# Zero-padding the first key tile of the value products, padding the first queries, and joining a unit's transposes in an attention + SwiGLU + SiLU kernel

## The chip, the cores and the metric

One core of one Trainium2 chip runs the whole program. The metric is the device time of one execution in microseconds (us); the kernel before has a median of 1140.44 us over three runs (1138.94 to 1141.12).

## What is computed

Three layers follow one another, all in float32.

- Forgetting attention with B = 4 batches, H = 8 heads, S = 576 positions, D = 64: `scores = q k^T / 8 + min(-(cum_i - cum_j), 0)` with `cum = cumsum(max(s, 0))`, a causal mask, a softmax, and the product with v.
- SwiGLU over the 2304 tokens x 512: `silu(x @ w_gate) * (x @ w_val) @ w_out` with an inner width of 1536.
- SiLU over the result: `silu(x @ w_in) @ w_out` with an inner width of 2048.

## The kernel before, in words

**Precision by parts.** Most matmuls run on operands of type fp32r, split into a high and a low part (`..h` and `..l`), so that one product is made of two or three matmuls. In the feed-forward layers these are lines 406 to 408 (high x high, high x low, low x high), always on the full array of 128 rows (contraction) by 128 columns (outputs), in spans of 288 tokens in the first layer. Only batch 0 keeps its attention weights whole in fp32 (`WHOLE_P`).

**Attention.** A sequence of 576 is cut into five tiles: the first has 64 positions, the others 128 (`TILES`). A unit is one half of one head: half A has the query tiles 0, 1, 2 (320 queries), half B the tiles 3 and 4 (256 queries). There are 64 units. Each goes through three stages, one slot apart:

- `a_scores` (L212), once per query tile: GpSimd makes the bias with its mask (L218, L221), TensorE the two score matmuls (L230; the first query tile has 64 queries and so a weight tile of 128 x 64), VectorE the sum with the minimum (L235), ScalarE the exponential (L241), and VectorE or GpSimd the normalization, into a buffer `e` (six of them).
- `a_transpose` (L250), once per group of key tiles (`GROUPS`: the first key tile alone, then tiles 1 and 2, then in half B tiles 3 and 4): transposes on TensorE (L264) of every query tile of the unit into one PSUM buffer `ptr`, then ScalarE takes the high part `ph` (L273) and VectorE the low part `pl` (L274). For the first key tile these have 64 rows.
- `a_pv` (L281): the value products (L292), two matmuls (`ph`, `pl`) for each key tile, all into one PSUM accumulator `pv`. The weights are the values with their high and low part side by side (128 columns): `vsa` for the first key tile, with 64 rows, `vsb` for the others, with 128. ScalarE and VectorE then join the two halves of the result (L306, L307).

PSUM has four buffers (`ps_a`) for all of attention's products: in each pair of slots scores, `pv` and `ptr` take 13 of them in turn, so that a tile takes over the buffer of the fourth one before it.

**Order.** After 18 slots of attention alone (batch 0 and a little of batch 1), chunks of the first feed-forward layer of batch b and slots of attention of batch b + 1 run interleaved: a chunk (`gv`, four steps of 24 matmuls, or `o1`, eight steps of 12) shares its steps out over the pieces of two slots (`slot_pieces`, L509). A slot's pieces are its scores, the split (L182) and load of the heads that follow, the value products of the unit two slots back, and the transposes of the unit one slot back, each group a piece of its own. The framework then fixes each engine's order at compile time, with a cost model of its own, so that it can put feed-forward matmuls ahead of a piece that would have to wait. In the first batch's chunks the weights are also decoded (`w_decode`, L364) on VectorE and ScalarE. The last batch's chunks and the second layer run without attention.

Of the kernel before, what the change touches and what calls it, by code (L numbers as in the profile page):

```python
# [8 lines left out]
F32 = mybir.dt.float32  # L9
F32R = mybir.dt.float32r  # L10
U32 = mybir.dt.uint32
AF = mybir.ActivationFunctionType
ALU = mybir.AluOpType
# [4 lines left out]
P = 128  # L18
# [49 lines left out]
def kernel(  # L68
# [15 lines left out]
    def pool(name, bufs, space=None, scope=ctx, side="left"):  # L84
        kw = {"space": space} if space is not None else {}
        return scope.enter_context(tc.tile_pool(name=name, bufs=bufs, side=side, reuse_waits="tile", **kw))
# [12 lines left out]
    qks_p = pool("qks", 2, scope=attention, side="right")  # L99
    cum_p = pool("cum", 2, scope=attention, side="right")  # L100
    e_p = pool("e", 6, scope=attention, side="right")
    pt_p = pool("pt", 4, scope=attention, side="right")
    v_p = pool("v", 2, scope=attention, side="right")
    xr_p = pool("xr", 2, scope=attention, side="right")
    xq_p = pool("xq", 2, scope=attention, side="right")
# [4 lines left out]
    def copy(eng, out, in_, scale=1.0):  # L110
        if eng == "a":
            nc.scalar.activation(out=out, in_=in_, func=AF.Copy, scale=scale)  # L112
        elif eng == "v":
            nc.vector.tensor_scalar(out=out, in0=in_, scalar1=scale, scalar2=None, op0=ALU.mult)
        else:
            nc.gpsimd.tensor_scalar(out=out, in0=in_, scalar1=scale, scalar2=1.0, op0=ALU.mult, op1=ALU.mult)
# [1 line left out]

    ident = const.tile([P, P], F32, name="ident")
    make_identity(nc, ident)  # L120
    cum = const.tile([B * H, S], F32, name="cum")
    cumq = const.tile([P, len(TILES), B * H], F32, name="cumq")
    cum_d = dram.tile([B * H, S], F32, name="cum_d")
    w32 = dram.tile([NGV + NO1, P, CW], F32, name="w32")
# [19 lines left out]


    st, loads = {}, []

    def a_load(b, h, halves):
        k1, v1, q0 = SPAN[halves]
# [28 lines left out]
    def a_split(b, h, halves):  # L178
        k1, v1, q0 = SPAN[halves]
        t, c, xa, xb = st.pop((b, h, halves))  # L180
        if (b, h) in WHOLE_S:
            ks, qs = t[:D, 1], (t[:D, 0],)  # L182
            q = t[:D, 0, q0:k1]
            nc.vector.tensor_scalar(out=q, in0=q, scalar1=-0.125, scalar2=None, op0=ALU.mult)
        else:
            ks = qks_p.tile([P, S], F32R, tag="ks", name="ks")
            qh = qks_p.tile([P, S], F32R, tag="qh", name="qh")
            ql = qks_p.tile([P, S], F32R, tag="ql", name="ql")
            qs = (qh, ql)
            copy(KHI[b], ks[:, :k1], t[:, 1, :k1])  # L190
            copy(QHI[b], qh[:, q0:k1], t[:, 0, q0:k1], -0.125)
            eng = nc.gpsimd if b in POOL_KS else nc.vector
            eng.tensor_tensor(out=ks[D:P, :k1], in0=t[D:P, 1, :k1], in1=ks[D:P, :k1].bitcast(F32), op=ALU.subtract)
            nc.vector.scalar_tensor_tensor(
                out=ql[:, q0:k1], in0=t[:, 0, q0:k1], scalar=-0.125, in1=qh[:, q0:k1].bitcast(F32),
                op0=ALU.mult, op1=ALU.subtract,
            )
        if (b, h) not in WHOLE_P:
            va_s = v_p.tile([64, 2, D], F32R, tag="vsa", name="vsa")
            vb_s = v_p.tile([P, 4, 2, D], F32R, tag="vsb", name="vsb")  # L200
            copy(VHI[b], va_s[:, 0, :], xa)
            copy(VHI[b], vb_s[:, :v1, 0, :], xb[:, :v1])
            nc.vector.tensor_tensor(out=va_s[:, 1, :], in0=xa, in1=va_s[:, 0, :].bitcast(F32), op=ALU.subtract)
            eng = nc.gpsimd if b in POOL_V else nc.vector
            eng.tensor_tensor(
                out=vb_s[:, :v1, 1, :], in0=xb[:, :v1], in1=vb_s[:, :v1, 0, :].bitcast(F32), op=ALU.subtract
            )
            xa, xb = va_s.rearrange("p t d -> p (t d)"), vb_s.rearrange("p j t d -> p j (t d)")
        for half in halves:
            st[b, h, half, "in"] = (ks, qs, c, xa, xb)  # L210

    def a_scores(b, h, half, i):  # L212
        ks, qs, c, _, _ = st[b, h, half, "in"]
        q0, r = TILES[i]
        wd = q0 + r
        hh = b * H + h
        e = e_p.tile([P, S], F32, tag="e", name="e")
        nc.gpsimd.tensor_scalar(  # L218
            out=e[:r, :wd], in0=c[:r, :wd], scalar1=-1.0, scalar2=cumq[:r, i, hh : hh + 1], op0=ALU.mult, op1=ALU.add
        )  # L220
        nc.gpsimd.affine_select(  # L221
            out=e[:r, q0:wd], in_=e[:r, q0:wd], pattern=[[-1, r]], compare_op=ALU.is_ge,
            fill=QMASK, base=0, channel_multiplier=1,
        )
        chunks = [(0, wd)] if wd <= 512 else [(0, wd // 2), (wd // 2, wd // 2)]
        m = None
        for c0, n in chunks:
            ps = ps_a.tile([P, 512], F32, tag="a", name="psc")
            for part, q in enumerate(qs):
                nc.tensor.matmul(  # L230
                    out=ps[:r, :n], lhsT=q[:, q0 : q0 + r], rhs=ks[:, c0 : c0 + n],
                    start=(part == 0), stop=(part == len(qs) - 1),
                )
            m2 = sm_p.tile([P, 1], F32, tag="m", name="m")
            nc.vector.tensor_tensor_reduce(  # L235
                out=e[:r, c0 : c0 + n], in0=ps[:r, :n], in1=e[:r, c0 : c0 + n], scale=1.0,
                scalar=3.0e38 if m is None else m[:r], op0=ALU.add, op1=ALU.min, accum_out=m2[:r],
            )
            m = m2
        l = sm_p.tile([P, 1], F32, tag="l", name="l")  # L240
        nc.scalar.activation(  # L241
            out=e[:r, :wd], in_=e[:r, :wd], func=AF.Exp, bias=m[:r], scale=-1.0, accum_out=l[:r]
        )
        rl = sm_p.tile([P, 1], F32, tag="rl", name="rl")
        nc.vector.tensor_scalar(out=l[:r], in0=l[:r], scalar1=1.0e-9, scalar2=None, op0=ALU.add)
        nc.vector.reciprocal(out=rl[:r], in_=l[:r])
        copy("v" if (b, i) in DVE_NORM else "g", e[:r, :wd], e[:r, :wd], rl[:r])
        st[b, h, "e", i] = e

    def a_transpose(b, h, half, js):  # L250
        tiles, base, n = HALF[half]
        ps = ps_a.tile([P, 512], F32, tag="a", name="ptr")
        kw = TILES[js[0]][1]
        at, put = 0, []
        for j in js:
            k0 = TILES[j][0]
            lo = max(k0, base)
            for i in tiles:
                q0, r = TILES[i]
                if q0 < k0:  # L260
                    continue
                e = st[b, h, "e", i]
                o = at + q0 - lo
                nc.tensor.transpose(ps[:kw, o : o + r], e[:r, k0 : k0 + kw], ident[:r, :r])  # L264
            put.append((j, at, lo - base, base + n - lo))
            at += base + n - lo
        ph = pt_p.tile([P, 512], F32 if (b, h) in WHOLE_P else F32R, tag="ph", name="ph")
        parts = (ph,)
        if (b, h) in WHOLE_P:
            copy("v" if (half, js[0]) in DVE_PT else "a", ph[:kw, :at], ps[:kw, :at])  # L270
        else:
            pl = pt_p.tile([P, 512], F32R, tag="pl", name="pl")
            nc.scalar.activation(out=ph[:kw, :at], in_=ps[:kw, :at], func=AF.Copy)  # L273
            nc.vector.tensor_tensor(  # L274
                out=pl[:kw, :at], in0=ps[:kw, :at], in1=ph[:kw, :at].bitcast(F32), op=ALU.subtract
            )
            parts = (ph, pl)
        for j, o, off, width in put:
            st[b, h, "p", half, j] = ([p[:kw, o : o + width] for p in parts], off, width)

    def a_pv(b, h, half):  # L281
        tiles, base, n = HALF[half]
# [226 lines left out]
    def slot_pieces(u):  # L509
        pcs = []  # L510
        if u < len(units):
            b, h, half, sp = units[u]
            for i in HALF[half][0]:
                pcs.append(lambda b=b, h=h, half=half, i=i: a_scores(b, h, half, i))
            if half == sp[0]:
                n = spans.index((b, h, sp))
                if n + 1 < len(spans):
                    pcs.append(lambda x=spans[n + 1]: a_split(*x))
                if n + 2 < len(spans):
                    pcs.append(lambda x=spans[n + 2]: a_load(*x))  # L520
        if u >= 2 and u - 2 < len(units):
            x = units[u - 2][:3]
            pcs.append(lambda x=x: a_pv(*x))
        if 1 <= u and u - 1 < len(units):
            b, h, half, _ = units[u - 1]
            for js in GROUPS[half]:
                pcs.append(lambda b=b, h=h, half=half, js=js: a_transpose(b, h, half, js))
        return pcs

    def w_ahead(c):  # L530
# [5 lines left out]

    def body():
        setup()
        a_load(*spans[0])
        a_load(*spans[1])  # L540
        a_split(*spans[0])
# [98 lines left out]
```

## Time and profile before

| | |
|---|---|
| median of three runs | 1140.44 us (1138.94 to 1141.12) |
| the profiled execution | 1141.18 us, of which the span from first to last instruction is 1139.4 us |
| busy in the span | TensorE 96%, VectorE 67%, GpSimd 54%, ScalarE 49% |
| chain that ended last | TensorE 73%, VectorE 6%, DMA 2%, issue 2%, ScalarE 1% |

How to read the rows further down: PE is TensorE's matmuls, PEld its weight loads, DVE is VectorE, ACT ScalarE, POOL GpSimd. A matmul's form is given as rows*columns of its weights, then the moving operand's shape: `64*128 64x320` contracts over 64 rows, gives 128 outputs, and streams 320 columns. Matmuls overlap and their ends are modelled, so what one costs is read from the start of one to the start of the next, not from its duration.

### The profile page before, as it was taken

The page shows a single profiled execution, that of the slowest core. Times are in us where ns is not written, and L with a number is a line of the kernel's source. Part 1 is how long each engine was busy: PE and PEld are TensorE (multiplying, and loading weights), DVE is VectorE, ACT ScalarE, POOL GpSimd, SP SyncE. Part 2 cuts the span into 40 slices and gives each one's busy share as a digit, 9 for nine tenths or more (in the row PEclk, how much of TensorE's full clock was granted, in tenths as well). Part 3 has the DMA queues.
Part 4 walks back from the last instruction along what each step waited for, and adds up shares of the span by engine and source line. Part 5 has one row for each costly group of instructions (what it writes and reads, how often), then busy time and mean ns, then how long its engine had stood idle before and what let it go on. Part 6 is the DMA issues. An engine that isn't in the chain of part 4 may idle for free.

```text
span 1139.4 us, 19549 instructions
## 1 busy us (share of the span) xinstructions
PE 1096.2 (96%) x6765; PEld 1000.2 (88%) x6765; DVE 764.8 (67%) x1776; ACT 561.0 (49%) x1242; POOL 615.9 (54%) x731
## 2 busy tenths in 40 slices
PE   7978988989999999999999999999999999999998
PEld 4656888888999999999999999889888898988887
DVE  6888998998877786777766435863463636454333
ACT  5876666655667655576744433455232323322221
POOL 4679889868877776686833543332333232223221
PEclk9988999999999999999999999999999999999999
DMA  5586565666343344333216222630111101000013
GB/s 141 136 244 215 175 193 189 182 173 196 119 119 113 109 117 144 113 101 101 69 54 217 75 84 84 202 109 25 50 51 43 57 19 56 19 1 1 1 51 116
DMA packets 53730, 121.41 MB, mean 107 GB/s; under 512 B 8256, under 2 KB 21568, under 8 KB 53632
## 3 DMA queue, kind: packets, MB, share of 16 engines
q1 hardware_dynamic: 53632, 120.17, 34.6%
q8 instruction: 53, 0.87, 0.3%
q14 instruction: 45, 0.37, 0.1%
HBM read 101.20 MB, written 18.95 MB: 105 GB/s over the span
## 4 chain that ended last, share of the span: by engine, by line
PE 73%; DVE 6%; DMA 2%; issue 2%; ACT 1%; POOL 0%; SPq 0%; DVEq 0%; ACTq 0%
PE po L406 9%; PE po L407 9%; PE po L408 9%; PE pgv L406 7%; PE pgv L407 7%; PE pgv L408 7%; PE pu L407 5%; PE pu L406 5%; PE pu L408 5%; PE pv L292 4%; PE ptr L264 3%; PE psc L230 2%; DVE dk L376 1%; DMA r<-in_w_dram 1%; DMA x2r<-x_d 1%
## 5 line engine op out<-in xcount | busy, mean ns | idle before, releaser
L421 POOL TENSOR_TENSOR h<-u,h 128x288 fp32r<-128x288 f32 (+2 forms) x176 | 187.1, 1064 | 332.5 <-ACT h L112 329.1
L406 PE MATMUL pgv<-xt,wh 128*128 128x288 f32 x768 | 233.7, 305 | 5.0 <-DVE u L417 3.5
L406 PE MATMUL po<-h,wh 128*128 128x288 f32 (+2 forms) x704 | 233.1, 333 | 3.7 <-DVE u L419 1.5
L407 PE MATMUL po<-h,wh 128*128 128x288 f32 (+2 forms) x704 | 232.6, 331 | 0.1
L408 PE MATMUL po<-h,wl 128*128 128x288 f32 (+2 forms) x704 | 232.3, 330 | 0.0
L408 PE MATMUL pgv<-xt,wl 128*128 128x288 f32 x768 | 230.0, 300 | 1.4 <-POOL wl L395 1.4
L407 PE MATMUL pgv<-xt,wh 128*128 128x288 f32 x768 | 230.0, 300 | 0.5 <-DVE xt L313 0.5
L395 POOL TENSOR_TENSOR wl<-wraw,wh 128x1024 fp32r<-128x1024 f32 x53 | 130.0, 2453 | 60.4 <-ACT wh L112 59.9
L406 PEld LDWEIGHTS pgv<-xt,wh 128*128 128x128 f32 x768 | 147.2, 192 | 6.7 <-DVE u L417 4.5
L408 PEld LDWEIGHTS pgv<-xt,wl 128*128 128x128 f32 x768 | 146.7, 191 | 1.8 <-POOL wl L395 1.8
L407 PEld LDWEIGHTS pgv<-xt,wh 128*128 128x128 f32 x768 | 147.1, 192 | 1.1 <-DVE xt L313 0.8
L218 POOL TENSOR_SCALAR e<-cumb,cumq 64x64 f32<-64x64 f32 (+4 forms) x160 | 112.4, 708 | 62.8 <-PE ptr L264 55.2
L406 PEld LDWEIGHTS po<-h,wh 128*128 128x128 f32 x704 | 132.0, 188 | 12.0 <-DVE u L419 2.0
L112 ACT ACTIVATE h<-u 128x288 fp32r<-128x288 f32 (+2 forms) x176 | 88.8, 508 | 102.2 <-DVE u L417 58.5
L408 PEld LDWEIGHTS po<-h,wl 128*128 128x128 f32 x704 | 132.2, 188 | 7.1
L407 PEld LDWEIGHTS po<-h,wh 128*128 128x128 f32 x704 | 132.2, 188 | 6.8 <-POOL h L421 0.5
L241 ACT ACTIVATE e<-e,m 64x64 f32<-64x64 f32 (+4 forms) x160 | 89.2, 558 | 95.9 <-DVE m L235 95.4
L417 DVE SCALAR_TENSOR_TENSOR u<-th,pu 128x464 f32<-128x464 f32 (+1 forms) x80 | 50.5, 631 | 122.3 <-ACT th L415 116.7
L501 DVE SCALAR_TENSOR_TENSOR acc<-po,acc 128x464 f32<-128x464 f32 (+1 forms) x140 | 88.7, 635 | 62.1 <-PE po L408 61.6
L415 ACT ACTIVATE th<-pu 128x464 f32<-128x464 f32 (+1 forms) x80 | 44.2, 552 | 174.0 <-PE pu L408 174.0
L112 ACT ACTIVATE wh<-wraw 128x1024 fp32r<-128x1024 f32 x88 | 92.2, 1053 | 56.0 <-PE po L407 32.1
L407 PE MATMUL pu<-x,wh 128*128 128x464 f32 (+1 forms) x320 | 118.9, 372 | 0.0
(83 smaller groups left out, 2189.3 us busy)
## 6 DMA issues: line engine op xcount, KB each, us to landing
wraw<-w SPq DMA_DIRECT2D x54, 512.0 KB, 4.0
r<-in_w_dram SPq DMA_DIRECT2D x52, 512.0 KB, 5.1
qkr<-in_qk_dram SPq DMA_DIRECT2D x64, 288.0 KB, 4.5
w<-wraw SPq DMA_DIRECT2D x18, 512.0 KB, 4.4
cumb<-cum_d SPq DMA_DIRECT2D x30, 288.0 KB, 3.4
r<-in_w_dram SPq DMA_DIRECT2D x32, 256.0 KB, 3.2
x_d<-acc SPq DMA_DIRECT2D x32, 144.0 KB, 3.8
vrb<-in_vb_dram SPq DMA_DIRECT2D x32, 128.0 KB, 3.6
```

Source lines behind the costliest of these rows:

```text
L112: nc.scalar.activation(out=out, in_=in_, func=AF.Copy, scale=scale)
L218: nc.gpsimd.tensor_scalar(out=e[:r, :wd], in0=c[:r, :wd], scalar1=-1.0, scalar2=cumq[:r, i, hh : hh + 1], op0=ALU.mult, op1=ALU.add)
L241: nc.scalar.activation(out=e[:r, :wd], in_=e[:r, :wd], func=AF.Exp, bias=m[:r], scale=-1.0, accum_out=l[:r])
L292: nc.tensor.matmul(out=acc[:rows, off : off + width], lhsT=vv, rhs=pp, start=(j == 0 and part == 0), stop=(j == js[-1] and part == len(ps) ...
L395: engines[eng].tensor_tensor(out=wl, in0=t, in1=wh.bitcast(F32), op=ALU.subtract)
L406: nc.tensor.matmul(out=ps[:, :n], lhsT=a, rhs=xh, start=(k == 0), stop=False)
L407: nc.tensor.matmul(out=ps[:, :n], lhsT=a, rhs=xl, start=False, stop=False)
L408: nc.tensor.matmul(out=ps[:, :n], lhsT=c, rhs=xh, start=False, stop=(k == last))
L415: nc.scalar.activation(out=th[:, :n], in_=pg[:, :n], func=AF.Tanh, scale=0.5)
L417: nc.vector.scalar_tensor_tensor(out=u, in0=th[:, :n], scalar=1.0, in1=pg[:, :n], op0=ALU.add, op1=ALU.mult)
L421: engines[LO[ph]].tensor_tensor(out=lo, in0=u, in1=hi.bitcast(F32), op=ALU.subtract)
L501: nc.vector.scalar_tensor_tensor(out=a, in0=ps[:, :n], scalar=0.5, in1=a, op0=ALU.mult, op1=ALU.add)
```

## The change

Four things are done. (1) For the batches whose weights are split, the first key tile's values (`vsa`) and weights (`ph`, `pl`) live in tiles of 128 rows whose upper 64 rows were filled with zeros once at the start by `zeros()` on GpSimd; the value products of that key tile then contract over 128 rows. These are three value tiles taken in turn and one pair of weight tiles for each half; the pool of the other `ph` and `pl` tiles has three buffers in place of four. (2) The score matmuls always take 128 query columns as weights, so the first query tile's do too, though only 64 rows of the result are read. (3) `a_transpose` issues all groups of a unit first and evicts them after, as one piece of the slot in place of two or three. (4) `cum` and the zeros' source `z` take buffers of the pool `e`.

```diff
-    pt_p = pool("pt", 4, scope=attention, side="right")
+    pt_p = pool("pt", 3, scope=attention, side="right")
+    zero_p = pool("zero", 1, scope=attention, side="right")
...
-    cum = const.tile([B * H, S], F32, name="cum")
+    cum = e_p.tile([B * H, S], F32, tag="e", name="cum")
...
+    first_v, first_p = [], []
+
+    def zeros():
+        z = e_p.tile([P, S], F32, tag="e", name="z")
+        nc.gpsimd.memset(z[D:P], 0.0)
+        for n in range(3):
+            va_s = zero_p.tile([P, 2, D], F32R, tag=f"v0_{n}", name="vsa")
+            copy("g", va_s[D:P], z[D:P, : 2 * D].rearrange("p (t d) -> p t d", t=2))
+            first_v.append(va_s)
+            if n == 2:
+                break
+            both = []
+            for part in "hl":
+                t = zero_p.tile([P, 320], F32R, tag=f"p{part}0_{n}", name=f"p{part}0")
+                copy("g", t[D:P], z[D:P, :320])
+                both.append(t)
+            first_p.append(both)
...
-            va_s = v_p.tile([64, 2, D], F32R, tag="vsa", name="vsa")
+            va_s = first_v[(b * H + h) % 3]
...
-            copy(VHI[b], va_s[:, 0, :], xa)
+            copy(VHI[b], va_s[:D, 0, :], xa)
...
-                    out=ps[:r, :n], lhsT=q[:, q0 : q0 + r], rhs=ks[:, c0 : c0 + n],
+                    out=ps[:, :n], lhsT=q[:, q0 : q0 + P], rhs=ks[:, c0 : c0 + n],
...
-    def a_transpose(b, h, half, js):
+    def a_transpose(b, h, half):
         tiles, base, n = HALF[half]
-        ps = ps_a.tile([P, 512], F32, tag="a", name="ptr")
...
+        done = []
+        for js in GROUPS[half]:
+            ps = ps_a.tile([P, 512], F32, tag="a", name="ptr")
...
+                    nc.tensor.transpose(ps[:kw, o : o + r], e[:r, k0 : k0 + kw], ident[:r, :r])
...
+            done.append((js, ps, kw, at, put))
+        for js, ps, kw, at, put in done:
+            whole = (b, h) in WHOLE_P
+            if js == (0,) and not whole:
+                ph, pl = first_p["AB".index(half)]
+                rows = P
...
+                st[b, h, "p", half, j] = ([p[:rows, o : o + width] for p in parts], off, width)
...
-            for js in GROUPS[half]:
-                pcs.append(lambda b=b, h=h, half=half, js=js: a_transpose(b, h, half, js))
+            pcs.append(lambda b=b, h=h, half=half: a_transpose(b, h, half))
...
         setup()
+        zeros()
```

## Rows read from the trace of the kernel before

**Rows 1.** Windows by stage: stretch, its length, busy us per engine (instructions).

```profile
0.00:118.00 118.00, 97.24 (x477) 69.11 (x477) 96.80 (x307) 82.27 (x209) 84.05 (x140) 0.91 0.65 185
118.00:262.00 144.00, 128.76 (x897) 119.10 (x896) 134.71 (x315) 86.35 (x199) 120.22 (x134) 0.98 0.62 185
262.00:608.00 346.00, 346.00 (x2559) 330.39 (x2558) 265.64 (x735) 209.09 (x513) 247.74 (x339) 1.00 0.37 111
608.00:1139.40 531.40, 524.20 (x2839) 481.64 (x2837) 267.65 (x423) 183.32 (x321) 163.88 (x120) 1.00 0.20 65
```

**Rows 2.** Chain that ended last by line, 262 to 608 us.

```profile
by line: PE pgv L406 15.5%; PE pgv L407 15.2%; PE pgv L408 15.2%; PE pv L292 13.5%; PE ptr L264 9.2%; PE po L406 7.8%; PE po L408 7.7%; PE po L407 7.7%; PE psc L230 7.4%; DMA x2r<-x_d 1.2%; DVE acc L449 0.1%; SPq L451 0.1%; issue 0.0%
```

**Rows 3.** Timeline of TensorE, half B's value products: start us, us, instruction.

```profile
525.95 0.29 PE L406 MATMUL po<-h,wh 128*128 128x288 f32 x1
...
526.22 0.29 PE L408 MATMUL po<-h,wl 128*128 128x288 f32 x1
526.43 0.38 PE L292 MATMUL pv<-ph,vsa 64*128 64x256 f32 x1
526.66 0.28 PE L292 MATMUL pv<-pl,vsa 64*128 64x256 f32 x1
526.86 0.38 PE L292 MATMUL pv<-ph,vsb 128*128 128x256 f32 x1
527.09 0.28 PE L292 MATMUL pv<-pl,vsb 128*128 128x256 f32 x1
...
527.56 0.28 PE L292 MATMUL pv<-pl,vsb 128*128 128x256 f32 x1
```

**Rows 4.** The same view, half A's value products, first and last.

```profile
262.83 0.29 PE L407 MATMUL pgv<-xt,wh 128*128 128x288 f32 x1
...
263.88 0.22 PE L292 MATMUL pv<-ph,vsb 128*128 128x128 f32 x1
```

**Rows 5.** The same, score matmuls of 320 columns.

```profile
534.56 0.31 PE L230 MATMUL psc<-ks,qh 128*128 128x320 f32 x1
534.70 0.31 PE L230 MATMUL psc<-ks,ql 128*128 128x320 f32 x1
```

**Rows 6.** Tile pv from 262 us: counts, min/median/max ns.

```profile
L292 PE MATMUL pv<-ph,vsa x36: 382/396/413, 263.1 to 600.8; 64*128 64x320 f32 x18, 64*128 64x256 f32 x18
```

**Rows 7.** Timeline of TensorE, the first query tile's scores.

```profile
388.04 0.19 PE L230 MATMUL psc<-ks,qh 128*64 128x64 f32 x1
...
388.34 0.29 PE L407 MATMUL pgv<-xt,wh 128*128 128x288 f32 x1
```

**Rows 8.** The same, the second query tile's scores.

```profile
280.61 0.25 PE L230 MATMUL psc<-ks,qh 128*128 128x192 f32 x1
...
280.96 0.29 PE L407 MATMUL po<-h,wh 128*128 128x288 f32 x1
```

**Rows 9.** The same, three transposes between feed-forward matmuls.

```profile
310.59 0.49 PE L264 MATMUL ptr<-ident,e 128*128 128x128 f32 x3
...
311.05 0.30 PE L407 MATMUL pgv<-xt,wh 128*128 128x288 f32 x1
```

**Rows 10.** The same, one transpose between feed-forward matmuls.

```profile
318.51 0.27 PE L264 MATMUL ptr<-ident,e 128*64 128x128 f32 x1
...
318.75 0.29 PE L408 MATMUL pgv<-xt,wl 128*128 128x288 f32 x1
```

**Rows 11.** Lines by form, GpSimd, first 12 us: count, busy, mean, idle before.

```profile
L218 POOL TENSOR_SCALAR e<-cumb,cumq 64x64 f32<-64x64 f32 x1 | 0.8, 753 | 7.0 <-ACT cumb L168 7.0
```

**Rows 12.** Timeline of all engines, value product's last matmul and its join.

```profile
282.63 0.28 PE L292 MATMUL pv<-pl,vsb 128*128 128x128 f32 x1
...
283.46 0.49 DVE L307 TENSOR_TENSOR x<-pv,xtmp 64x320 f32<-64x320 f32 x1
```

**Rows 13.** The same, another unit.

```profile
309.04 0.28 PE L292 MATMUL pv<-pl,vsb 128*128 128x128 f32 x1
...
313.78 0.41 DVE L307 TENSOR_TENSOR x<-pv,xtmp 64x256 f32<-64x256 f32 x1
```

More of the change, by code (lines that the diff above doesn't have):

```diff
@@ L198, in a_split @@
         if (b, h) not in WHOLE_P:
-            va_s = v_p.tile([64, 2, D], F32R, tag="vsa", name="vsa")
+            va_s = first_v[(b * H + h) % 3]
             vb_s = v_p.tile([P, 4, 2, D], F32R, tag="vsb", name="vsb")
-            copy(VHI[b], va_s[:, 0, :], xa)
+            copy(VHI[b], va_s[:D, 0, :], xa)
             copy(VHI[b], vb_s[:, :v1, 0, :], xb[:, :v1])
-            nc.vector.tensor_tensor(out=va_s[:, 1, :], in0=xa, in1=va_s[:, 0, :].bitcast(F32), op=ALU.subtract)
+            nc.vector.tensor_tensor(out=va_s[:D, 1, :], in0=xa, in1=va_s[:D, 0, :].bitcast(F32), op=ALU.subtract)
             eng = nc.gpsimd if b in POOL_V else nc.vector
@@ L248, in a_scores @@
         st[b, h, "e", i] = e
-    def a_transpose(b, h, half, js):
+    def a_transpose(b, h, half):
         tiles, base, n = HALF[half]
-        ps = ps_a.tile([P, 512], F32, tag="a", name="ptr")
[L253 to L279, printed above, removed]
@@ new lines, in a_transpose @@
+        done = []
+        for js in GROUPS[half]:
+            ps = ps_a.tile([P, 512], F32, tag="a", name="ptr")
+            kw = TILES[js[0]][1]
+            at, put = 0, []
+            for j in js:
+                k0 = TILES[j][0]
+                lo = max(k0, base)
+                for i in tiles:
+                    q0, r = TILES[i]
+                    if q0 < k0:
+                        continue
+                    e = st[b, h, "e", i]
+                    o = at + q0 - lo
+                    nc.tensor.transpose(ps[:kw, o : o + r], e[:r, k0 : k0 + kw], ident[:r, :r])
+                put.append((j, at, lo - base, base + n - lo))
+                at += base + n - lo
+            done.append((js, ps, kw, at, put))
@@ new lines, in a_transpose @@
+        for js, ps, kw, at, put in done:
[3 more added lines that the diff above has]
+                rows = P
+            else:
+                ph = pt_p.tile([P, 512], F32 if whole else F32R, tag="ph", name="ph")
+                pl = None if whole else pt_p.tile([P, 512], F32R, tag="pl", name="pl")
+                rows = kw
+            parts = (ph,)
+            if whole:
+                copy("v" if (half, js[0]) in DVE_PT else "a", ph[:kw, :at], ps[:kw, :at])
+            else:
+                nc.scalar.activation(out=ph[:kw, :at], in_=ps[:kw, :at], func=AF.Copy)
+                nc.vector.tensor_tensor(
+                    out=pl[:kw, :at], in0=ps[:kw, :at], in1=ph[:kw, :at].bitcast(F32), op=ALU.subtract
+                )
+                parts = (ph, pl)
+            for j, o, off, width in put:
+                st[b, h, "p", half, j] = ([p[:rows, o : o + width] for p in parts], off, width)
```

## The prediction

> **What bounds the kernel now.** I read the windows by stage first [rows 1]. They cut the span in four. In the first 118 us (attention of batch 0) no engine is full. From 118 to 262 us VectorE, which also decodes weights there, is busy for 134.71 of 144 us (94%), and TensorE stands idle for 15.2. From 262 to 608 us TensorE is busy for all of 346.00 us, at the full clock (1.00, the level of 2.4 GHz), while VectorE has 265.64 and GpSimd 247.74. After 608 us there is no attention left, and the change touches nothing. The chain of waits agrees for the third stage: of what ended last, only TensorE's lines have more than 1.2% [rows 2]. So a microsecond of TensorE's queue between 262 and 608 us is a microsecond of the kernel; elsewhere it probably is not.
>
> A busy PE says nothing of whether its pipeline is full. For that I read the timeline from start to start. Between feed-forward matmuls of 288 columns lie (526.22 - 525.95) / 2 = 0.135 us (below I write 0.13); value products of 256 columns on `vsb` follow one another at (527.56 - 527.09) / 4 = 0.118. Around the two products on `vsa`, whose form is 64*128, four gaps are longer: feed-forward to the first `vsa` 0.21, first to second 0.23, `vsa` to `vsb` 0.20, first `vsb` to its second 0.23 [rows 3]. Two of these four gaps stand at the passage between forms of 64 and of 128 rows, and two behind the first matmul after it. The last two `vsb` of the same accumulation, with the same columns and the same kind of weights, show none of it. So the price hangs on the change of rows, twice in each unit.
>
> **Part 1, zero rows in the value products.** After the change every value product is 128*128. Half B: from the feed-forward matmul at 526.22 to the second regular `vsb` at 527.21 (527.09 + 0.118) takes 0.99 us; at regular gaps it would be 0.13 + 4 x 0.118 = 0.60. Saved: 0.39 us [rows 3]. Half A: 263.88 - 262.83 = 1.05 us [rows 4]; at regular gaps 0.13 + 2 x 0.14 (320 columns, [rows 5]) + 2 x 0.118 = 0.65. Saved: 0.40. I take 0.39 for both. From 262 us on there are 36 of these units [rows 6], so **36 x 0.39 = 14.0 us**. Twice 64 rows more in a weight tile add no column and no instruction. The remaining 12 of 48 units lie in the stage of VectorE: at most 12 x 0.39 = 4.7 us, at least nothing. TensorE waits there for VectorE's results, and VectorE gets none of its work taken away, so I take 0 and keep 4.7 for the range.
>
> Here two rules of the Trainium skill stand against each other. The page "TensorE: Matmul & The Clock Gate" (Why this matters for your kernels) has a single matmul over 32 rows take as long as one over 128, so that rows as such are worth nothing; by it alone the padding saves 0 and the sum would be the cost of part 2. The page "TensorEngine Tiling (Array Packing)" (Tiling Modes, Key Properties) says that a change of the tiling mode drains the engine; by it the padding saves something, of a size that it doesn't give. The trace bears out the second: 0.20 to 0.23 us where 0.12 to 0.13 is regular.
>
> **Part 2, first queries padded to 128.** The two score matmuls of the first query tile (64 columns, weights 128*64) cost 388.34 - 388.04 - 0.13 = 0.17 us of TensorE's time, the feed-forward matmul behind them at its regular gap taken off [rows 7]. Those of the second tile, with full weights and 192 columns, cost 280.96 - 280.61 - 0.13 = 0.22 [rows 8]. 192 columns are well under 256, which take 0.118 each, and yet each takes 0.11: it is not the columns streamed that set this, so the padded tile should pay the same. Cost: 0.05 us a head, for 18 heads (36 units) **0.9 us**. Bounds: 0 if 64 columns stay as cheap as now; and a gain of 18 x 0.17 = 3.1 if they vanish, which nothing suggests. A change of columns (128 to 64) shows no long gap as a change of rows does: a transpose of 128*64 costs 0.11 (below), the same as one of 128*128.
>
> **Part 3, the transposes together.** Three transposes between feed-forward matmuls cost 311.05 - 310.59 - 0.13 = 0.33 us [rows 9], one alone 318.75 - 318.51 - 0.13 = 0.11 [rows 10]: three times one, so no cost of entering or leaving a group is there to be saved. 0 us. The transposes over the first 64 queries keep their form of 64*64 and so their change of rows in half A; that stays. Each group already needs all of the unit's `e` (the first key tile concerns every query), so no transpose starts on less than before. An eviction now stands behind all groups' transposes, 9 x 0.11 = 1.0 us for half B at the most, and its reader, the value product, comes a slot later. I take 0; what can go wrong here is the slower rival.
>
> **Part 4, the rest.** `zeros()` is one fill and seven copies on GpSimd at the start. GpSimd idles there for 7.0 us until the first `cumb`, and an elementwise instruction of that region takes 0.75 us [rows 11]: 8 x 0.75 = 6.0, an upper bound, since the copies have 128 or 320 columns on half the rows. Covered; without the cover up to 6 us. Three `ph`/`pl` buffers serve three tiles a pair of units where four served five: no tighter for split batches. For batch 0, still five tiles a pair, it is tighter, but the value product that frees a buffer stands ahead of the transposes on TensorE's queue. No DMA is added, removed or moved past SP's queue. For the first 118 us I take 0, with one transpose's 0.11 us for each of 16 units, 1.8 us, either way.
>
> **Sum.** The profiled execution took 1141.18 us. 1141.18 - 14.0 + 0.9 = 1128.1. It stands 0.74 above the median of the runs, so 1127.3 is what I forecast for the median. Its own range is 1124 to 1131 (0 to 1.8 either way at the start, some of part 2's bounds, a little of the early 4.7).
>
> **The rivals.**
>
> *All 48 units pay.* The early stage alternates between VectorE and TensorE, and its gaps close too: another 4.7 - 6 x 0.05 = 4.4 us, 1122.9. For it: TensorE is busy 89% there. Against: VectorE's 94%. 0.12.
>
> *VectorE takes half of it back.* With 13 us less, VectorE's 265.64 us fall in 333 us, 80%, and unevenly; its low parts (L274) or sums (L235) come late and TensorE starts to wait. Half of 13.1 lost gives 1133.9. Against: TensorE has no wait at all in that stage today. 0.14.
>
> *Rows cost nothing.* If the long gaps belong to what is read (`ph` and `pl` of the first group, the most recent tiles) and not to the rows, only part 2 is left: 1140.44 + 0.9 = 1141.3. For it: no run has shown the padded form. Against: the first `vsb` has the same delay as the second `vsa`. This is also where the first of the two rules above, on the page "TensorE: Matmul & The Clock Gate" of the Trainium skill, would end. 0.04.
>
> *A score waits for the accumulator (slower).* In a four-step chunk the old 14 pieces fell as 3, 4, 3, 4, the value products in the second step and half B's first score in the third, at least some feed-forward matmuls later. The new 11 fall as 2, 3, 3, 3, and the third step holds value products, half B's transposes and that score, which takes over the buffer of `pv`, four tiles back. The buffer is free when VectorE has joined the halves (L307), between 283.95 - 282.63 = 1.3 us [rows 12] and 314.19 - 309.04 = 5.2 us [rows 13] after the last value product; nine transposes cover 1.0. A wait of 0.3 to 4.2 us, 2.2 in the middle, in two thirds of 18 pairs: 12 x 2.2 = 26 us, 1153. It decides from 13.1 / 12 = 1.1 us a pair. Against: the order is fixed with feed-forward matmuls put ahead of what must wait, as in the stage that is full now. 0.06.
>
> **How the numbers follow.** The forecast has 0.64. A measurement here can tell about 0.2% (2.3 us) from no change. Faster: 0.64 + 0.12 + 0.14 = 0.90; same: 0.04; slower: 0.06. The range runs from the first rival with the start's 1.8 and some of part 2's bound (1119) to the second with the same on top (1137), and leaves out the last two cases and the far ends of the others.
>
> **What would show it.** In the changed kernel's timeline no value product of split batches has 64 rows, and from the feed-forward matmul ahead of half B's products to the fifth product it takes 0.60 us in place of 0.99. The first query tile's two scores take 0.22 in place of 0.17. The third stage shrinks by about 13 us with TensorE still without a wait; the second and the last keep their length. I am wrong if the gaps of 0.20 to 0.23 remain with 128 rows, if TensorE gets waits on `pv`'s or `ptr`'s readers in the third stage, or if the first 118 us move by more than 2.

## The result and the profile after

The changed kernel has a median of 1129.25 us (1128.46 to 1130.13, 4 runs) beside 1140.78 us for the kernel before: a ratio of 0.9902, 95% interval 0.9885 to 0.9919. Two further sets of runs of the same pair, on chips 4 and 12, gave 0.9889 (0.9873 to 0.9905) and 0.9891 (0.9875 to 0.9907). The profiled execution took 1128.86 us with a span of 1126.7.

To compare stages of equal work, I count feed-forward matmuls from the first: the stage below begins with the start of the 961st and ends with the start of the 2497th, in every kernel of this text. In the kernel before these lie at 307.4 and 601.5 us. Windows by stage, the kernel before (columns: stretch, its length, busy time and instructions of PE, PEld, DVE, ACT, POOL, granted clock, DMA share, GB/s):

```profile
262.00:307.40 45.40, 45.40 (x337) 43.30 (x336) 35.90 (x112) 28.90 (x72) 36.15 (x56) 1.00 0.54 152
307.40:601.50 294.10, 294.10 (x2175) 280.58 (x2174) 225.83 (x617) 179.05 (x440) 208.92 (x283) 1.00 0.34 103
601.50:1139.40 537.90, 530.70 (x2888) 488.14 (x2887) 271.56 (x428) 184.46 (x325) 166.54 (x122) 1.00 0.20 67
```

The same view of the changed kernel:

```profile
118.00:262.00 144.00, 129.62 (x898) 122.40 (x897) 134.67 (x308) 85.78 (x197) 123.68 (x132) 0.95 0.60 183
262.00:305.20 43.20, 42.25 (x323) 41.36 (x323) 36.14 (x108) 27.39 (x70) 36.74 (x56) 1.00 0.59 163
305.20:589.10 283.90, 283.44 (x2176) 279.66 (x2175) 216.50 (x619) 177.66 (x441) 204.01 (x284) 1.00 0.37 107
589.10:1126.70 537.60, 530.35 (x2889) 488.42 (x2887) 272.95 (x429) 185.04 (x324) 167.32 (x122) 1.00 0.20 67
```

Of 12.7 us of span, 10.2 (294.1 to 283.9) fall in that one stage, with the same feed-forward matmuls, value products and transposes in it, and two score matmuls more after the change. The tail, 537.9 and 537.6, hardly changed. The other 2.2 us were gained ahead of it. In the stretch from 118 to 262 us VectorE is as busy as before (134.67 beside 134.71, [rows 1]).

The timeline of TensorE in the changed kernel, half B's value products (to be laid beside [rows 3]):

```profile
433.27 0.29 PE L435 MATMUL po<-h,wh 128*128 128x288 f32 x1
433.40 0.28 PE L321 MATMUL pv<-ph,vsa 128*128 128x256 f32 x1
433.52 0.28 PE L321 MATMUL pv<-pl,vsa 128*128 128x256 f32 x1
433.64 0.28 PE L321 MATMUL pv<-ph,vsb 128*128 128x256 f32 x1
433.76 0.28 PE L321 MATMUL pv<-pl,vsb 128*128 128x256 f32 x1
433.88 0.28 PE L321 MATMUL pv<-ph,vsb 128*128 128x256 f32 x1
```

All four long gaps are gone: from the feed-forward matmul to the fifth product 433.88 - 433.27 = 0.61 us, where it was 0.99. The first query tile's scores, by contrast, cost more (to be laid beside [rows 7]):

```profile
419.96 0.19 PE L249 MATMUL psc<-ks,qh 128*128 128x64 f32 x1
419.99 0.27 PE L249 MATMUL psc<-ks,ql 128*128 128x64 f32 x1
420.10 0.38 PE L435 MATMUL pgv<-xt,wh 128*128 128x288 f32 x1
420.32 0.30 PE L436 MATMUL pgv<-xt,wh 128*128 128x288 f32 x1
```

420.32 - 419.96 - 0.13 = 0.23 us beside 0.17: the padded tile pays what the second query tile pays. The Trainium skill's page "TensorE: Matmul & The Clock Gate" (LDWEIGHTS) says that loading weights takes time by their columns and not by their rows. The weight loads in the trace of the kernel before agree on both sides (mean ns in the second figure behind the bar):

```profile
L292 PEld LDWEIGHTS pv<-pl,vsb 128*128 128x128 f32 x144 | 27.2, 189 | 0.0
L292 PEld LDWEIGHTS pv<-pl,vsa 64*128 64x128 f32 x48 | 9.0, 188 | 0.2 <-issue 0.2
L230 PEld LDWEIGHTS psc<-ks,ql 128*128 128x128 f32 x160 | 32.3, 202 | 0.1
L230 PEld LDWEIGHTS psc<-ks,ql 128*64 128x64 f32 x32 | 4.5, 141 | 0.0
```

64 rows more make no difference to a load (188 and 189 ns), 64 columns more do (141 and 202). Loads overlap matmuls, so only 0.06 us for two matmuls is left of that in the pace.

`zeros()` stands on GpSimd where no one waits (timeline of GpSimd in the changed kernel, first and last of its eight instructions, and the first bias):

```profile
1.36 0.57 POOL L153 MEMSET z<- 64x576 f32 x1
...
5.49 0.31 POOL L117 TENSOR_SCALAR vsa<-z 64x128 fp32r<-64x128 f32 x1
8.31 1.68 POOL L237 TENSOR_SCALAR e<-cumb,cumq 64x64 f32<-64x64 f32 x3 [2.51 <-ACT cumb L187]
```

It ends at 5.8 us, and the first bias begins at 8.31. Before, GpSimd waited 7.04 us for that `cumb`; now the rest of this wait is 2.51.

### The profile page after: what moved, and what is told of

Same layout as the page of the kernel before. It is cut to its first block, busy times and chain, and to the rows that moved or that the text cites. A ratio compares the mean times of both kernels' runs of the same rounds, so it can differ in the third digit from the quotient of the medians.

```text
span 1126.7 us, 19576 instructions
## 1 busy us (share of the span) xinstructions
PE 1085.5 (96%) x6765; PEld 1001.7 (89%) x6765; DVE 755.7 (67%) x1776; ACT 559.5 (50%) x1242; POOL 622.9 (55%) x739
## 4 chain that ended last, share of the span: by engine, by line
PE 73%; DVE 5%; POOL 2%; issue 2%; ACT 1%; DMA 1%; SPq 0%; DVEq 0%; POOLq 0%
PE po L435 9%; PE po L436 9%; PE po L437 9%; PE pgv L436 7%; PE pgv L435 7%; PE pgv L437 6%; PE pu L436 6%; PE pu L435 6%; PE pu L437 6%; PE ptr L285 3%; PE pv L321 3%; PE psc L249 2%; DMA x2r<-x_d 1%; DVE dk L405 1%; POOL wl L424 1%
## 5 line engine op out<-in xcount | busy, mean ns | idle before, releaser
L450 POOL TENSOR_TENSOR h<-u,h 128x288 fp32r<-128x288 f32 (+2 forms) x176 | 192.0, 1092 | 341.3 <-ACT h L113 337.3
L436 PE MATMUL pu<-x,wh 128*128 128x464 f32 (+1 forms) x320 | 118.9, 372 | 0.0
L435 PE MATMUL pu<-x,wh 128*128 128x464 f32 (+1 forms) x320 | 118.8, 371 | 0.0
```

The costliest lines, as they stand in the source:

```text
L435: nc.tensor.matmul(out=ps[:, :n], lhsT=a, rhs=xh, start=(k == 0), stop=False)
L436: nc.tensor.matmul(out=ps[:, :n], lhsT=a, rhs=xl, start=False, stop=False)
L450: engines[LO[ph]].tensor_tensor(out=lo, in0=u, in1=hi.bitcast(F32), op=ALU.subtract)
```

## The experiments

### 64 rows again, and nothing else

```diff
-                rows = P
+                rows = kw
...
-            xa, xb = va_s.rearrange("p t d -> p (t d)"), vb_s.rearrange("p j t d -> p j (t d)")
+            xa, xb = va_s[:D].rearrange("p t d -> p (t d)"), vb_s.rearrange("p j t d -> p j (t d)")
```

> The changed kernel, but the value products of the first key tile read only the lower 64 rows of the same tiles; every instruction and its place in every engine's order stays the same. My theory (a change of rows on TensorE costs two long gaps into and two out of these products, 0.39 us a unit, and only the 36 units of the stage in which TensorE is full pay for it): the gaps of 0.20 to 0.23 us come back and the time rises from 1129.25 by about 36 x 0.38 = 13.7 us, to 1143. If all 48 units pay: 1147.5. Rival (the gaps belonged to what is read and to its buffers, and these are now other buffers): 1129, as the changed kernel.

Measured: 1142.14 us, 1.0001 of before (0.9992 to 1.001). This is the cleanest of the runs, since every engine has the same instructions in the same order as in the changed kernel, and only the rows that 96 matmuls and their weight loads read differ. The whole gain is gone. Windows by stage and the timeline of this kernel:

```profile
305.30:600.70 295.40, 295.29 (x2176) 281.43 (x2175) 216.51 (x620) 179.26 (x441) 203.76 (x284) 1.00 0.36 102
```

```profile
438.33 0.29 PE L435 MATMUL po<-h,wh 128*128 128x288 f32 x1
438.56 0.38 PE L321 MATMUL pv<-ph,vsa 64*128 64x256 f32 x1
438.78 0.28 PE L321 MATMUL pv<-pl,vsa 64*128 64x256 f32 x1
438.99 0.38 PE L321 MATMUL pv<-ph,vsb 128*128 128x256 f32 x1
439.21 0.28 PE L321 MATMUL pv<-pl,vsb 128*128 128x256 f32 x1
439.33 0.28 PE L321 MATMUL pv<-ph,vsb 128*128 128x256 f32 x1
```

1.00 us in place of 0.61, with the gaps in the same four places as in [rows 3]. The rival that the gaps hung on the buffers falls, and with it the prediction's rival of the name *Rows cost nothing*: rows as such cost nothing (128 rows keep the regular 0.12 us), but their change does. The stage tells more: it is 295.4 - 283.9 = 11.5 us longer, and it *begins* at 305.3 us, where the changed kernel's begins at 305.2. So the 17 units ahead of it, most with their long gaps, cost nothing that shows: all of them would be 6.6 us, and the changed kernel's own profiles begin this stage up to 1.1 us apart. I had expected 36 units to pay; 31 did (the count from 305.2 us in the changed kernel, tile `pv`):

```profile
L321 PE MATMUL pv<-ph,vsa x31: 277/281/310, 306.0 to 588.8; 128*128 128x256 f32 x16, 128*128 128x320 f32 x15
```

Between the two traces, matched instruction by instruction, each of the 31 units differs by 0.385 to 0.399 us, half A as half B: 12.0 in all. 11.5 were measured, and the rest is a wait of 0.5 us that the changed kernel has in this stage (shown below) and this one has not.

### 64 rows in batch 1 alone

```diff
-                rows = P
+                rows = kw if b == 1 else P
...
-            xa, xb = va_s.rearrange("p t d -> p (t d)"), vb_s.rearrange("p j t d -> p j (t d)")
+            xa, xb = va_s[: D if b == 1 else P].rearrange("p t d -> p (t d)"), vb_s.rearrange("p j t d -> p j (t d)")
```

> As the run with 64 rows, but in batch 1 alone, whose 16 units have their value products between 109.8 and 290 us in the changed kernel's trace, 12 of them ahead of 262 us. My theory (a unit ahead of 262 us costs the kernel nothing, since VectorE sets the pace there): 4 x 0.38 = 1.5 us, 1130.8. Rival (every unit pays wherever it lies): 16 x 0.38 = 6.1 us, 1135.4.

Measured: 1129.49 us, 0.9891 of before (0.9877 to 0.9905), again with the same order on every engine. The changed kernel's three ratios are 0.9902, 0.9889 and 0.9891. Batch 1's 16 units can do without the zero rows, and the rival in which every unit pays (0.995) is out. My own 1130.8 (0.991) lies just above the interval too: the four units behind 262 us, for which I had added 1.5 us, cost nothing either. The full stage has the changed kernel's length to the digit:

```profile
305.90:589.80 283.90, 283.44 (x2177) 279.66 (x2175) 216.28 (x619) 177.67 (x441) 204.16 (x284) 1.00 0.36 106
```

### The first queries unpadded, twice

```diff
-                    out=ps[:, :n], lhsT=q[:, q0 : q0 + P], rhs=ks[:, c0 : c0 + n],
+                    out=ps[:r, :n], lhsT=q[:, q0 : q0 + r], rhs=ks[:, c0 : c0 + n],
```

> The changed kernel with the first query tile's score matmuls back at 64 query columns. My theory (the padding costs 0.05 to 0.06 us a head, for 18 heads): 1.0 us faster, 1128.2, with an order of instructions that differs and may blur it by 1 us. Rival (the padding saves a change of form as the zero rows do, two long gaps of 0.1 us a head): 18 x 0.2 = 3.6 us slower, 1132.9.

Measured: 1126.84 us, 0.9863 (0.9845 to 0.9881).

> The changed kernel with the first query tile's scores at 64 query columns, now beside the changed kernel itself. If its first ratio (0.9863) came from the 15 heads' 0.06 to 0.1 us that the trace shows: 1 to 1.5 us under the changed kernel. If its order of instructions is better by itself: 3 to 4 us under it.

Measured: 1128.36 us, 0.9869 (0.9848 to 0.9889), beside 1129.39 us and 0.9891 for the changed kernel on the same chip, of which was expected:

> The changed kernel as the base on this chip: 0.989 to 0.990 of before.

Unpadded is not slower, so the padding saves nothing. Windows of the full stage, without the padding:

```profile
305.20:587.70 282.50, 282.50 (x2176) 278.92 (x2176) 214.89 (x619) 177.70 (x441) 204.36 (x284) 1.00 0.37 107
```

282.5 beside 283.9: 1.4 us, of which 0.8 are 14 heads at 0.06 and 0.5 a wait that the changed kernel has in this stage and this one has not, the one for `x`, in which VectorE joins the halves of a value product (waits of TensorE from 262 to 600 us, changed kernel: in total, times, longest; the other two lie ahead of the stage):

```profile
PE psc L249 <- DVE l L264: 0.6, 1, 0.6
PE psc L249 <- DVE x L336: 0.5, 1, 0.5
PE ptr L285 <- DVE m L254: 0.3, 1, 0.3
```

The medians, 1.0 us apart beside each other, agree in sign but their intervals overlap.

### The transposes as separate pieces

```diff
-    def a_transpose(b, h, half):
+    def a_transpose(b, h, half, groups):
...
-        for js in GROUPS[half]:
+        for js in groups:
...
-            pcs.append(lambda b=b, h=h, half=half: a_transpose(b, h, half))
+            for js in GROUPS[half]:
+                pcs.append(lambda b=b, h=h, half=half, js=js: a_transpose(b, h, half, [js]))
```

> The changed kernel with each group of a unit's transposes as its own piece again, evicted behind its own transposes. My theory (joining them saves TensorE nothing, three cost three times one): 1129 within 1.5, the rest being order. Rival 1 (a group pays for being entered and left, 0.1 us each): one more group in half A and two in half B, 18 x 0.3 = 5.4 us slower, 1134.6. Rival 2 (joining holds three PSUM buffers and made waits): faster by more than 1.5.

Measured: 1128.40 us, 0.9881 (0.9868 to 0.9895). Joining saves nothing, and a group doesn't pay for being entered and left. In the full stage the separate pieces are even 1.4 us shorter (282.5 beside 283.9, below). 0.5 of this is the wait for `x`, which this kernel does not have, so the second rival is borne out that far; and two score matmuls fewer fall in the stage (about 0.3). The rest I did not take apart, since the order on every engine differs.

### The zero rows alone

The two diffs above together. The changed kernel was run beside it as the base.

> The changed kernel once more, as the base of the three runs beside it: 0.990 of the time of before, as at first.

> Of the change only the zero rows and their buffers: the first query tile's scores have 64 query columns again and each group of transposes is a piece of its own. My theory (the zero rows carry the gain; the query padding costs 1.0 to 1.4 us, the joining saves nothing): 1 to 2.5 us under the changed kernel of this call. Rival (each of the two other parts carries some of the gain): over the changed kernel.

Measured: 1128.55 us, 0.9885 (0.9868 to 0.9901), beside 1128.39 us, 0.9889 (0.9873 to 0.9905) for the changed kernel. My theory asked for 1 to 2.5 us less, and the median doesn't show it; the rival asked for more, and it doesn't show that either. The trace of one execution says where it went there. Windows of the full stage with separate pieces, and of this kernel, and a wait of TensorE between 586 and 620 us of this kernel:

```profile
305.40:587.90 282.50, 282.50 (x2175) 279.37 (x2174) 223.99 (x616) 178.47 (x438) 210.66 (x283) 1.00 0.35 107
```

```profile
304.70:586.40 281.70, 281.70 (x2174) 278.56 (x2173) 224.78 (x616) 178.29 (x438) 210.20 (x283) 1.00 0.36 107
```

```profile
PE pgv L435 <- DVE u L446: 3.2, 1, 3.2
```

The stage is 2.2 us shorter than the changed kernel's 283.9, as expected. Then, where the last feed-forward chunks of the first layer meet the loads of the second, one gate matmul waits 3.2 us for VectorE and gives it back; the changed kernel's three profiles wait 0.8, 1.7 and 0.5 us there. The profiled execution was the slowest of its four (1129.75 us; the others 1128.21 to 1128.75), so it is not shown that the others lose their gain in the same way. What is saved ahead of such a meeting counts only if the meeting still works out.

### The transposes on 128 rows too, twice

One change of rows was left in the changed kernel: the transposes of the first 64 queries (64*64). Since the padded scores already give 128 rows, the whole first tile can be worked on for 128, and its transposes write 128 columns, of which the next tile's write the upper 64 anew.

```diff
     for i, (q0, r) in enumerate(TILES):
         pt = ps_a.tile([P, 512], F32, tag="a", name=f"pcum{i}")
+        r = P
...
-        wd = q0 + r
+        wd, w, r = q0 + r, r, P
...
-            out=e[:r, q0:wd], in_=e[:r, q0:wd], pattern=[[-1, r]], compare_op=ALU.is_ge,
+            out=e[:r, q0:wd], in_=e[:r, q0:wd], pattern=[[-1, w]], compare_op=ALU.is_ge,
...
                     o = at + q0 - lo
+                    r = P
                     nc.tensor.transpose(ps[:kw, o : o + r], e[:r, k0 : k0 + kw], ident[:r, :r])
```

> The changed kernel, in which the first query tile is worked on for all 128 rows that its padded scores already give (mask, exponential, sum, normalization, on as many columns as before), and its transposes take 128 rows and write 128 columns, whose upper half the next query tile's transposes write again. No transpose with 64 rows is left. My theory (any change of rows costs two long gaps in and out, here 0.517 us for the three transposes of half A's first group against 0.33 for three full ones, in the 15 or so half-A units behind 305 us): 0.19 x 15 = 2.8 us faster than the changed kernel. Rival (the gaps are a matter of the value products' accumulation, not of rows as such): no change beyond 1 us.

Measured: 1127.42 us, 0.9877 (0.9863 to 0.9892); the changed kernel beside it 0.9889.

> The changed kernel with full transposes, a second time beside it. The transposes' own saving is 15 x 0.184 = 2.8 us in the stage where TensorE is full; the first time 1.0 us of it reached the median. 1 to 3 us under the changed kernel if the loss ahead of that stage was chance; 0 to 1 if it belongs to this order.

Measured: 1126.12 us, 0.9857 (0.9841 to 0.9874); the changed kernel beside it 0.9891 (0.9875 to 0.9907). Both times it has the lowest median of the kernels that ran together, 1.0 and 3.3 us under the changed one. By the ratios to before (0.9877 and 0.9857) it is not told apart from the kernel with the first queries unpadded (0.9863 and 0.9869), which did not run beside it the first time. The full stage is the same in both profiles, which began it at 307.2 and at 303.9 us:

```profile
307.20:587.60 280.40, 280.40 (x2177) 279.65 (x2176) 216.19 (x620) 177.24 (x442) 206.32 (x284) 1.00 0.38 109
```

```profile
303.90:584.30 280.40, 280.40 (x2177) 279.66 (x2176) 216.15 (x620) 177.26 (x442) 206.21 (x284) 1.00 0.38 109
```

3.5 us less than 283.9: the 2.8 expected, and the changed kernel's wait of 0.5 for `x` is gone. The timelines show it in one group of transposes, first in the changed kernel, then in this one:

```profile
380.96 0.29 PE L435 MATMUL pgv<-xt,wh 128*128 128x288 f32 x1
381.18 0.58 PE L285 MATMUL ptr<-ident,e 64*64 64x64 f32 x3
381.52 0.38 PE L436 MATMUL pgv<-xt,wh 128*128 128x288 f32 x1
381.73 0.30 PE L437 MATMUL pgv<-xt,wl 128*128 128x288 f32 x1
```

```profile
327.72 0.29 PE L437 MATMUL pgv<-xt,wh 128*128 128x288 f32 x1
327.85 0.49 PE L287 MATMUL ptr<-ident,e 128*64 128x128 f32 x3
328.10 0.38 PE L438 MATMUL pgv<-xt,wh 128*128 128x288 f32 x1
328.32 0.29 PE L439 MATMUL pgv<-xt,wl 128*128 128x288 f32 x1
```

0.77 us and 0.60 from feed-forward to the second feed-forward matmul behind, though this one streams 64 columns more. The gap into the group falls from 0.22 to 0.13. So the cost is not one of value products alone: it goes with the change of rows in transposes too. One more run had this edit and the separate pieces of transposes together:

> As the run with full transposes, with each group of transposes as its own piece: by the run with separate pieces 0 to 2 us under that run; 3 to 5 us under the changed kernel of this call. If the separate pieces were only a matter of order, within 1 us of the run with full transposes.

Measured: 1128.89 us, 0.9885 (0.9865 to 0.9906), inside the interval of the run without the pieces (0.9863 to 0.9892) and of the changed kernel. Neither expectation came true: it is 0.5 us above the changed kernel beside it and 1.5 above the run without the pieces, and the intervals leave nothing to choose by.

Where the two profiles of the same kernel differ by 3.3 us is ahead of 304 us, in the stretch in which TensorE waits for results of VectorE and GpSimd. There the same program varies by as much from one execution to the next, and so a part of 1 us can't be read from these medians.

## Why the prediction was right, point by point

**The bound.** Right in kind, off in place. A shorter product pays only where TensorE's queue sets the pace; the tail, which has no attention, is unchanged. But the stage in which a unit pays begins at about 305 us and not at 262. I had taken the first moment from which TensorE was busy without a gap [rows 1]. That it was busy showed only that it had just enough to do: with shorter products it has gaps there (42.25 of 43.20), and the run with 64 rows reaches 305 us at the same time with none of the saving. The first 118 us moved by about 1 us, inside the 2 that I had set: the 97th feed-forward matmul starts at 119.26 us before and at 118.19 after.

**Part 1, the zero rows.** The price of a unit was right: 0.39 worked out from [rows 3, 4], 0.39 gone in the traces. The number of paying units was the mis-sized factor: 36 forecast, 31 found, 11.5 us measured by the run with 64 rows where 14.0 stood in the sum. That the early units are worth nothing was right, and holds for more of them than I thought (batch 1 alone). The rule of the Trainium skill's page "TensorEngine Tiling (Array Packing)" (Tiling Modes, Key Properties), that a change of the tiling mode drains the engine, agrees with these runs for a change of rows: 1.00 us beside 0.61 with nothing else changed. A change of columns alone shows no such time (0.13 us into a group of `128*64` transposes). The trace gives the rows and columns of a matmul and not its tiling mode, so the time is shown, and that a drain is the reason for it is not.

**Part 2, the padded queries.** Right: +0.05 forecast, 0.23 - 0.17 = 0.06 measured, with no gain.

**Part 3, the joined transposes.** I took 0. The stage is 1.4 us shorter without the joining and the medians don't tell them apart; no gain is there. The rival in which a score waits for the accumulator came to one wait of 0.5 us on `x` in the whole stage, in place of 26: the sign of being wrong that I had named did show, too small to matter. The rival in which VectorE takes half back is out as well, since TensorE waits for nothing else in that stage.

**Part 4, the zeros.** Right: eight instructions, 4.4 us, inside the wait for the first `cumb`.

**The sum.** 1127.3 was forecast and 1129.25 measured, inside its own range of 1124 to 1131. The third stage was to shrink by about 13 us. By the stage of equal work it is 10.2: 31 units give 11.5, and 1.3 go back (295.4 with 64 rows beside 294.1 before), of which 0.8 are the padding and about 0.3 the two score matmuls more in the stage. Another 2.2 us came ahead of 305 us, which no term of the sum had. So the total came out close partly by luck: 2.5 us too much for the units, and 2.2 from elsewhere in their place. These are not the rows, since the run with 64 rows has them too, nor the padding or the joining, since the kernel with the zero rows alone begins the stage at 304.7. The changed kernel's own three profiles begin it at 305.2, 306.2 and 306.3 us; there is one profile of before. Whether this comes of the buffers, of the new order or of chance is open.

## What to carry to other kernels

Where matmuls of different contraction heights share TensorE's queue, read the gaps from start to start around the odd ones: a busy engine hides them. Padding the short tile with zero rows that are written once cost no time on TensorE here; padding the weight's columns did. And count as paying only what lies where the engine stays full after the change too: a stretch that is just full is no bound, and a run that undoes one factor in one batch alone shows it.

## What the runs showed of the hardware that was not expected

That a change of rows costs about 0.1 us at the passage and as much again before the second matmul behind it, nearly 0.4 for a visit of two matmuls, was read from [rows 3] and is now shown. What I did not expect is that it need not cost the kernel anything even where TensorE is busy without a gap: in the kernel before it was busy for all 45.40 us from 262 to 307.4, and the units there paid nothing that shows. As expected, a change of the weight's columns from 128 to 64 at 128 rows showed no such gap, and with weights of 128 columns two matmuls of 64 streamed columns cost 0.23 us, about as much as two of 192 (0.22): from 64 to 192 columns it is not the streamed columns that set the pitch.
